# First batch of a fused attention and feed-forward kernel: k and q loaded as rows, normalised there, turned by TensorE

## The chip, the cores and the metric

One core of one Trainium2 chip runs the whole program. Its engines are TensorE (PE, with its weight loads PEld), VectorE (DVE), ScalarE (ACT), GpSimd (POOL) and SyncE (SP), which here issues every DMA, one after the other. The metric is the device time of one execution in microseconds; the kernel before took 1610.94 us (median of 3 runs, 1608.66 to 1612.02).

## The reference

Inputs: q, k, v of 8 batches x 12 heads x 448 tokens x 64 numbers, two gains of 64 numbers, and the weights of a feed-forward layer (768 x 2048 and 2048 x 768, float64 in DRAM, so that each weight has to be put together from two 32-bit halves on the core). Cut to what matters:

```python
q_n = q / sqrt(mean(q*q, -1) + 1e-6) * g_q      # the same for k with g_k
scores = q_n @ k_n.T / 8                         # per batch and head, 448 x 448
attn = softmax(scores)                           # max subtracted, sum + 1e-9
x = (attn @ v) as [8*448 tokens, 12*64]
h = x @ w_in
out = (s * relu(h)**2 + b) @ w_out               # 3584 x 768
```

## The kernel before, in words

**Precision.** TensorE multiplies in fp32r; where that is not enough a number is split into a rounded high part and the rest, and two or three products are added up. So k lies on 128 partitions as its high part (64 rows) over its low part (`ka`), q twice as its high part (`qa`), and the low part of q stands in `qb`, with one more row for the negated maximum of each query; `kb` is the high part of k with a row of ones.

**Pairs and slots.** The 96 heads are worked in 48 pairs (6 pairs are one batch); `j` is the head within a pair. The first part of the program is one loop over slots. A slot does one 128-key chunk of one head: two matmuls into `st` (`score_t`, L343 and L346), its exponent on ACT (L358 in the first batch, L362 later), and two slots later its product with v (`weigh`, L402). A pair has W = 8 slots, so slot 0 to slot 383 are attention. Ten slots ahead (AHEAD) a slot also makes one 112-query block of plain scores `sh` (L305), whose row maximum DVE takes (L316).

**What each pair needs first.** A table `jobs` says in which slot, counted from the pair's first slot s0 = 8p (s1 = s0 + 4j), each preparation stands: `load` brings k and q of the pair as rows (`raw`, 448 KB), `norm` squares them on ACT (L242), sums on DVE (L247) and raises the mean to -1/2 on POOL (L249, L250); `keep` writes these 1/rms to DRAM, `spread` reads them back onto all 128 partitions (`rb`, 448 KB for each head), `load_kq` brings k and q of a head a second time, already turned and on 128 partitions (`kq`, 448 KB), `scale` multiplies the two (L267, L268) and `split_kq` makes `ka`, `qa`, `qb` (L286 to L290). `double_kb` copies the high part of k into `kb` by a DMA, `shift` puts the maxima into `qb` by a DMA, `take`, `gather` and `divide` (L427 to L443) form the softmax's division through DRAM, `split_x` makes the operand of the feed-forward layer.

**The rest.** `convert` turns the 24 pieces of w_in (512 KB each) from float64 into a high and a low part: one load (L119), two ACT instructions, four on DVE, one on POOL. PACE lists the slots in which it goes on. Its load buffer `w64` exists once. From slot START + 48b on, `filler` gives TensorE the feed-forward matmuls of the batch just finished, FILL = (2, 2, 2) of them in each slot (L175); before the first such slot TensorE has attention alone. `rectify` takes their sums out (L192) and stores them (L194). After the loop the last batch's w_in matmuls run while w_out is converted, and then all the w_out matmuls (L621).

**What sets the order.** In the first part all five engines run in exactly the order in which the program is written (`manual_schedule`), SP among them: an instruction that waits holds up all behind it on its engine. Within a slot the order is: `score_t`, two filler matmuls, the last exponent's split, the exponent, jobs begun in an earlier slot, the jobs of this slot in order of the pair, the plain score and two filler matmuls, `rectify`, `split_e_lo`, the maximum, the weight pieces, `weigh`, two filler matmuls.

Of the kernel before, what the change touches and what calls it, by code (L numbers as in the profile page):

```python
# [23 lines left out]
START = 16  # L24
# [3 lines left out]
FIRST = -31  # L28
# [3 lines left out]
PACE = (-24, *range(2, 62, 5), *range(60, 93, 3))  # L32
# [5 lines left out]
def attention_then_relu2_ffn(  # L38
# [3 lines left out]
    kq_rows: bass.AP,  # L42
    v: bass.AP,
# [6 lines left out]
):  # L50

# [14 lines left out]
    nc = tc.nc  # L66
# [120 lines left out]
    def rectify():  # L187

        while later:
            ph, bank, b, fc = later.pop(0)  # L190
            r = xp.tile([P, SEQ], F32, tag="r", bufs=2, name=f"r{b}_{fc}")
            S.activation(r, ph[:, :SEQ], AF.Relu)  # L192
            free.append(bank)
            nc.sync.dma_start(r_d[b][fc], r)  # L194

    with tc.tile_pool(name="apool", bufs=1) as ap:
        raws, kqs, invs, vrs, nmxs, shs = ({} for _ in range(6))
        sts, movers, avs, uzs, zts, zbs, us = ({} for _ in range(7))

        def load(p):  # L200
            raw = raws[p] = ap.tile([P, 2, TILES, D], F32, tag="raw", name=f"raw{p}")
            nc.sync.dma_start(raw, kq_rows[p])

# [60 lines left out]
        def scale(p, j):  # L264
            t, rb = kqs[p, j], invs.pop((p, j))
            engine = V if p < NP else G
            engine.tensor_tensor(t[:, 0], t[:, 0], rb[:, 0], ALU.mult)  # L267
            V.scalar_tensor_tensor(t[:, 1], t[:, 1], gqk, rb[:, 1], ALU.mult, ALU.mult)  # L268
# [13 lines left out]
        def split_kq(p, j):  # L282

            t, n = kqs.pop((p, j)), p % 2
            a = slice(j * SEQ, (j + 1) * SEQ)
            S.copy(ka[n][:, a], t[:, 0])  # L286
            S.copy(qa[n][:, a], t[:, 1])
            G.tensor_tensor(ka[n][D:, a], t[D:, 0], ka[n][D:, a].bitcast(F32), ALU.subtract)  # L288
            engine = V if p < NP else G
            engine.tensor_tensor(qb[n][:D, a], t[:D, 1], qa[n][:D, a].bitcast(F32), ALU.subtract)  # L290
# [81 lines left out]
        def split_e_lo(i):  # L372
            p, j, kc, rows = chunk(i)
            if p < NP:
                return
            st, bank = sts.pop(i)
            ah = movers[i][0]
            if kc < 3:
                al = ap.tile([P, SEQ], F32R, tag="al", bufs=3, name=f"al{i}")
                movers[i].append(al)  # L380
            else:
                al = ah[rows:]
            V.tensor_tensor(al, st[:rows, :SEQ], ah[:rows].bitcast(F32), ALU.subtract)  # L383
            free.append(bank)
# [135 lines left out]
        for i, s_ in enumerate(chain((-29,), PACE)):  # L520
            for n in range(1 + 3 * (i > 0)):
                at(s_ + n, next, converted, None)
# [9 lines left out]
        with tc.manual_schedule(engines=ORDERED):  # L532
            begun = []
            for s_ in range(FIRST, NSLOT + START + 1):
                if s_ == FIRST + 3:
# [5 lines left out]
                if s_ in (-28, -20, -13):  # L541
                    warm_up(30)
# [7 lines left out]
                begun = [g for g in begun if next(g, 0) is None]  # L550
                for f, a in jobs[s_]:
# [26 lines left out]
            rectify()  # L578


    with tc.tile_pool(name="opool", bufs=2) as op:
# [57 lines left out]
        with tc.manual_schedule(engines=ORDERED - {ENGINE.SP}):  # L639
# [4 lines left out]
            for m in range(NFC + NFC // NS):  # L644
# [8 lines left out]
                for step in range(4):  # L653
                    for g in now:
                        next(g)
                    if step == 1:
                        rectify()
                    if step == 2:
# [54 lines left out]
```

## Time and profile before

| what | value |
|---|---|
| median of 3 runs | 1610.94 us |
| profiled execution, its own time | 1612.49 us |
| its span on the core | 1610.7 us |
| mean granted TensorE clock | 0.956 |
| PE busy over the span | 1477.9 us, 92% |
| DVE, ACT, POOL busy | 58%, 50%, 46% |
| first feed-forward matmul starts | 227.8 us |

The page's strip of 40 slices is about 40 us a slice: the first five or six slices, the slots without feed-forward matmuls, are the ones in which PE is not at 9. In rows of the timeline the first two numbers are the start in the span and the duration, and the bracket at the end is the idle time of the engine just before with what ended it. In rows of waits the three numbers are the total, how often, and the longest. In the table by windows the numbers are busy us of each engine, then the granted clock, the DMA share and GB/s.

### The profile page before, as it was taken

How to read it: one execution, taken by the hardware profiler on the slowest of the kernel's cores; microseconds unless marked ns; L12 is line 12 of the kernel's file. 1: busy time of each engine (PE TensorE's matmuls, PEld its weight loads, DVE VectorE, ACT ScalarE, POOL GpSimd, SP SyncE). 2: the span in 40 equal slices, each digit the busy share in tenths (PEclk: the TensorE clock that was granted, in tenths of full speed). 3: DMA queues.
4: the chain of work that ended last, by engine and by line, in shares of the span. 5: the costliest groups of instructions: out<-in, count | busy, mean ns of one | idle time of the engine just before them, and what ended most of it. 6: DMA issues, size and time to landing. Idle time of an engine off the chain costs nothing. (4 is left out here: it accounts for less than half of the span.)

```text
span 1610.7 us, 21747 instructions
## 1 busy us (share of the span) xinstructions
PE 1477.9 (92%) x7344; PEld 1354.8 (84%) x7344; DVE 939.8 (58%) x1405; ACT 804.8 (50%) x1504; POOL 743.0 (46%) x599
## 2 busy tenths in 40 slices
PE   6666558999999999999999999999799999999998
PEld 6444447989989989989888989998699999999998
DVE  4687778677777777777677767349943222222210
ACT  2444546666666667666666666525632222222210
POOL 5456666767767767767666766115620000000000
PEclk8878779999999999999999999999899999999999
DMA  5666646665665666656656654166633323232310
GB/s 172 192 187 194 177 139 181 200 187 175 186 184 183 183 181 182 187 177 187 182 177 183 184 179 140 55 190 196 185 108 97 84 82 99 72 108 73 90 38 30
DMA packets 226240, 241.92 MB, mean 150 GB/s; under 512 B 74832, under 2 KB 201808, under 8 KB 226128
## 3 DMA queue, kind: packets, MB, share of 16 engines
q1 hardware_dynamic: 226128, 240.53, 50.3%
q8 instruction: 58, 0.95, 0.3%
q14 instruction: 54, 0.44, 0.1%
HBM read 188.22 MB, written 40.89 MB: 142 GB/s over the span
## 5 line engine op out<-in xcount | busy, mean ns | idle before, releaser
L175 PE MATMUL ph<-x,wih 128*128 128x448 f32 x1536 | 491.8, 368 | 0.0
L175 PEld LDWEIGHTS ph<-x,wih 128*128 128x128 f32 x1536 | 292.9, 191 | 23.5
L362 ACT ACTIVATE st<-st 128x448 f32<-128x448 f32 x336 | 176.9, 526 | 255.5 <-PE st L346 253.5
L316 DVE TENSOR_REDUCE nmx<-sh 112x1 fp32r<-112x448 f32 x384 | 236.9, 618 | 111.9 <-PE sh L305 109.0
L175 PE MATMUL ph<-x,wil 128*128 128x448 f32 x768 | 285.9, 372 | 0.0
L621 PE MATMUL po<-woh,gh 128*128 128x384 f32 x896 | 231.3, 337 | 10.3 <-ACT gh L608 8.7
L621 PE MATMUL po<-wol,gh 128*128 128x384 f32 x896 | 230.8, 337 | 2.0 <-POOL wol L134 2.0
L621 PE MATMUL po<-woh,gl 128*128 128x384 f32 x896 | 229.7, 337 | 1.0 <-DVE gl L609 1.0
L402 PE MATMUL av<-ah,vs 128*128 128x448 f32 x672 | 197.4, 376 | 12.5 <-ACT ah L370 7.6
L305 PE MATMUL sh<-ka,qa 128*112 128x448 f32 x384 | 150.1, 394 | 55.7 <-POOL ka L288 49.9
L288 POOL TENSOR_TENSOR ka<-kq,ka 64x448 fp32r<-64x448 f32 x96 | 114.6, 1194 | 175.7 <-ACT ka L286 170.9
L383 DVE TENSOR_TENSOR al<-st,ah 128x448 fp32r<-128x448 f32 x252 | 155.1, 616 | 60.3 <-ACT ah L370 60.3
L370 ACT CAST ah<-st 128x448 fp32r<-128x448 f32 x336 | 179.1, 533 | 2.4
L621 PEld LDWEIGHTS po<-woh,gh 128*128 128x128 f32 x896 | 163.5, 190 | 12.0 <-ACT gh L608 9.3
L621 PEld LDWEIGHTS po<-wol,gh 128*128 128x128 f32 x896 | 163.5, 190 | 3.2 <-POOL wol L134 3.2
L305 PEld LDWEIGHTS sh<-ka,qa 128*112 128x112 f32 x384 | 107.8, 282 | 69.2 <-POOL ka L288 60.7
L343 PE MATMUL st<-qa,ka 128*128 128x448 f32 (+1 forms) x384 | 165.0, 430 | 1.0 <-DVE nmx L316 1.0
L621 PEld LDWEIGHTS po<-woh,gl 128*128 128x128 f32 x896 | 163.1, 189 | 1.4 <-DVE gl L609 1.4
L175 PEld LDWEIGHTS ph<-x,wil 128*128 128x128 f32 x768 | 146.5, 191 | 12.2
L346 PE MATMUL st<-qb,kb 128*128 128x448 f32 (+1 forms) x384 | 147.0, 383 | 2.2 <-DMA qb<-nmx 2.2
L402 PEld LDWEIGHTS av<-ah,vs 128*128 128x128 f32 x672 | 129.8, 194 | 22.8 <-ACT ah L370 13.3
L603 ACT ACTIVATE r<-r 128x2048 f32<-128x2048 f32 x28 | 53.7, 1917 | 172.1 <-DMA r<-r_d 172.1
(66 smaller groups left out, 2125.2 us busy)
## 6 DMA issues: line engine op xcount, KB each, us to landing
kq<-in_dram SPq DMA_DIRECT2D x96, 448.0 KB, 4.1
rb<-i_d SPq DMA_DIRECT2D x96, 448.0 KB, 5.0
r_d<-r SPq DMA_DIRECT2D x128, 224.0 KB, 3.8
r<-r_d SPq DMA_DIRECT2D x24, 1024.0 KB, 5.9
raw<-in_dram SPq DMA_DIRECT2D x48, 448.0 KB, 4.8
w64i<-in_dram SPq DMA_DIRECT2D x24, 512.0 KB, 4.9
w64o<-in_dram SPq DMA_DIRECT2D x48, 256.0 KB, 3.1
kb<-ka SPq DMA_DIRECT2D x96, 112.0 KB, 2.8
```

The costliest lines, as they stand in the source:

```text
L175: T.matmul(ph[:, :SEQ], w[:, cc, f0 : f0 + P], xs[b, cc][:, part, :], start=n == 0, stop=n == 3 * NCC - 1,)
L288: G.tensor_tensor(ka[n][D:, a], t[D:, 0], ka[n][D:, a].bitcast(F32), ALU.subtract)
L305: T.matmul(sh[:QC, :SEQ], qa[p % 2][:, a].rearrange("k (p c) -> k c p", c=NQ)[:, c], ka[p % 2][:, a], start=True, stop=True,)
L316: V.tensor_reduce(out=nmxs[p][:, c : c + 1], in_=sh[:QC, :SEQ], op=ALU.max, axis=AX.X, negate=True)
L343: T.matmul(st[:rows, :SEQ], ka[n][:, keys], qa[n][:, q], start=True, stop=False)
L346: T.matmul(st[:rows, :SEQ], kb[n][:, keys], qb[n][:, q], start=False, stop=True,)
L362: S.activation(st[:rows, :SEQ], st[:rows, :SEQ], AF.Exp)
L370: S.copy(ah[:rows], sts[i][0][:rows, :SEQ])
L383: V.tensor_tensor(al, st[:rows, :SEQ], ah[:rows].bitcast(F32), ALU.subtract)
L402: T.matmul(av[:, :SEQ], x, a, start=kc == 0 and m == 0, stop=kc == 3 and m == len(todo) - 1,)
L603: S.activation(r, r, AF.Square)
L621: T.matmul(po[e][0][:, :HALF], x[:, fc, :], w[:, f, e * HALF : (e + 1) * HALF], start=fc == 0 and m == 0, stop=fc == NFC - 1 and m == 2,)
```

## The change

- For the six pairs of the first batch k and q are loaded once, as rows of a new input `rows0` (112 partitions, 224 KB for each head, `load_rows`). `norm_rows` squares on ACT into another tile, sums on DVE, forms 1/rms on POOL for 112x8 numbers and multiplies the rows by it on POOL. `turn` lets TensorE transpose the eight 112x64 blocks of a head into two PSUM tiles; `split_turned` makes `ka`, `qa`, `qb` from PSUM with three ACT and two DVE instructions (the gain goes in there). `load`, `norm`, `keep`, `load_kq`, `spread`, `scale` and `split_kq` are no longer done for these pairs; later pairs keep them.
- For later pairs `load_kq` and `spread` stand one slot later by the table, and `double_kb` one slot later for all.
- The four steps of `divide` move from s0 + 14, 15, 18, 21 to s0 + 13, 14, 16, 18. START goes from 16 to 13, FIRST from -31 to -22, and PACE's slots move with them by one for most pieces. Only two groups of warm-up matmuls of 30 remain of three.
- The stores of `r` are issued at the start of the jobs of the next slot (`keep_r`), no longer right behind the ACT instruction that makes `r`.
- The low part `al` of an exponent has two buffers, before three (the squares of `norm_rows` use them as well).

```diff
-START = 16
+START = 13
-FIRST = -31
+FIRST = -22
-PACE = (-24, *range(2, 62, 5), *range(60, 93, 3))
+PACE = (-17, *range(1, 61, 5), *range(59, 92, 3))
...
             S.activation(r, ph[:, :SEQ], AF.Relu)
             free.append(bank)
+            kept.append((b, fc, r))
+    def keep_r():
+        while kept:
+            b, fc, r = kept.pop(0)
             nc.sync.dma_start(r_d[b][fc], r)
...
+        def load_rows(p, j):
+            tag = f"{('kq', 'rb')[p % 2]}{j}"
+            raw = raws[p, j] = ap.tile([QC, 2, NQ, D], F32, tag=tag, name=f"rows{p}_{j}")
+            nc.sync.dma_start(raw, rows0[p, :, j])
+        def norm_rows(p, j):
+            raw = raws[p, j].rearrange("p t c d -> p (t c) d")
+            n = 2 * NQ
+            sq = ap.tile([QC, n, D], F32, tag="al", bufs=2, name=f"sq{p}_{j}")
+            S.activation(
+                sq.rearrange("p i d -> p (i d)"), raw.rearrange("p i d -> p (i d)"), AF.Square
+            )
+            yield
+            ssq = ap.tile([QC, n], F32, tag="ssq", bufs=2, name=f"ssq{p}_{j}")
+            V.tensor_reduce(out=ssq, in_=sq, op=ALU.add, axis=AX.X)
+            ri = ap.tile([QC, n], F32, tag="ri", bufs=2, name=f"ri{p}_{j}")
+            G.tensor_scalar(ri, ssq, 1.0 / D, 1e-6, ALU.mult, ALU.add)
+            G.tensor_tensor(ri, ri, mhalf[:QC, :n], ALU.pow)
+            G.tensor_tensor(raw, raw, ri.unsqueeze(2).broadcast_to([QC, n, D]), ALU.mult)
+        def turn(p, j):
+            raw = raws.pop((p, j))
+            for t in range(2):
+                tk, bank = psum(f"tk{p}_{j}_{t}")
+                for c in range(NQ):
+                    T.transpose(
+                        tk[:D, c * QC : (c + 1) * QC], raw[:, t, c], ident[:QC, :QC]
+                    )
+                tks[p, j, t] = tk[:D, :SEQ], bank
+        def split_turned(p, j):
+            n, a = p % 2, slice(j * SEQ, (j + 1) * SEQ)
+            (k, k_bank), (q, q_bank) = (tks.pop((p, j, t)) for t in range(2))
+            S.copy(ka[n][:D, a], k)
+            S.activation(qa[n][:D, a], q, AF.Copy, scale=gqk[:D])
+            S.activation(qa[n][D:, a], q, AF.Copy, scale=gqk[:D])
+            yield
+            V.tensor_tensor(ka[n][D:, a], k, ka[n][:D, a].bitcast(F32), ALU.subtract)
+            V.scalar_tensor_tensor(
+                qb[n][:D, a], q, gqk[:D], qa[n][:D, a].bitcast(F32), ALU.mult, ALU.subtract
+            )
+            free.extend((k_bank, q_bank))
...
-                al = ap.tile([P, SEQ], F32R, tag="al", bufs=3, name=f"al{i}")
+                al = ap.tile([P, SEQ], F32R, tag="al", bufs=2, name=f"al{i}")
...
-            at(s0 - 30, load, p)
-            at(s0 - 26, norm, p)
-            at(s0 - 22, keep, p)
+            if p >= NP:
+                at(s0 - 30, load, p)
+                at(s0 - 26, norm, p)
+                at(s0 - 22, keep, p)
...
-                at(s1 - 19 if p else -27, load_kq, p, j)
-                at(s1 - 19 if p else -19, spread, p, j)
-                at(s1 - 14, scale, p, j)
-                at(s1 - 12, split_kq, p, j)
-                at(s1 - 11, double_kb, p, j)
+                if p >= NP:
+                    at(s1 - 18, load_kq, p, j)
+                    at(s1 - 18, spread, p, j)
+                    at(s1 - 14, scale, p, j)
+                    at(s1 - 12, split_kq, p, j)
+                else:
+                    at(max(s1 - 28, FIRST), load_rows, p, j)
+                    at(s1 - 20, norm_rows, p, j)
+                    at(s1 - 13, turn, p, j)
+                    at(s1 - 12, split_turned, p, j)
+                at(s1 - 10, double_kb, p, j)
...
-            at(s0 + 14, divide, p, 0)
-            at(s0 + 15, divide, p, 1)
-            at(s0 + 18, divide, p, 2)
-            at(s0 + 21, divide, p, 3)
+            at(s0 + 13, divide, p, 0)
+            at(s0 + 14, divide, p, 1)
+            at(s0 + 16, divide, p, 2)
+            at(s0 + 18, divide, p, 3)
...
-                if s_ in (-28, -20, -13):
+                if s_ in (FIRST, FIRST + 4):
                     warm_up(30)
```

How the rows move shows at two places. The first is ACT at the program's start. Before (raw is a pair's rows, kq a head turned, wih and w64i a piece of w_in):

```order
L242 ACTIVATE raw_211<-raw_211 128x896
L123 ACTIVATE wih_213<-w64i_215 128x512
L133 CAST wih_213<-wai_216 128x512
L123 ACTIVATE wih_213<-w64i_265 128x512
L242 ACTIVATE raw_270<-raw_270 128x896
L286 CAST ka_190<-kq_0_251 128x448
L287 CAST qa_192<-kq_0_251 128x448
```

Of the changed kernel (rows_0 and rows_1 are the two heads of a pair, tk what TensorE has turned):

```order
L225 ACTIVATE sq_0_253<-rows_0_244 112x512
L125 ACTIVATE wih_248<-w64i_250 128x512
L225 ACTIVATE sq_1_298<-rows_1_246 112x512
L135 CAST wih_248<-wai_251 128x512
L125 ACTIVATE wih_248<-w64i_302 128x512
L249 CAST ka_190<-tk_0_0_318 64x448
L250 ACTIVATE qa_192<-tk_0_1_323,gqk 64x448
L251 ACTIVATE qa_192<-tk_0_1_323,gqk 64x448
L225 ACTIVATE sq_0_331<-rows_0_255 112x512
```

The first split of k (L286, now L249) stood behind two pairs' squares and the second piece of w_in; it now stands behind two heads' squares and the same second piece.

The second place is SP (the DMA queue) in a later batch, over the steps that lead to the division of pair 15 (zt15 gathered, z_d15 written). Before:

```order
L435 DMA zb14_3623<-z_d14_96 64x448 x2
L293 DMA qb1_197<-nmx17_3526 1x112x4
L253 DMA i_d19_149<-ri19_3545 128x2x7
L202 DMA raw20_3632<-in_1_dram 128x896
L194 DMA r_d1_75<-r1_5_3638 128x448
L419 DMA zt15_3515<-uz15_1_3626 64x1x7
L293 DMA kb0_194<-ka0_190 64x448
L206 DMA kq19_0_3709<-in_0_dram 128x2x448
L262 DMA rb19_0_3711<-i_d19_149 128x2x448
L194 DMA r_d1_75<-r1_6_3717 128x448
L293 DMA qb1_197<-nmx17_3526 1x112x4
L431 DMA z_d15_97<-zt15_3515 128x7
```

Of the changed kernel:

```order
L308 DMA i_d19_149<-ri19_3663 128x2x7
L212 DMA raw20_3752<-in_1_dram 128x896
L204 DMA r_d1_75<-r1_6_3758 128x448
L472 DMA zt15_3628<-uz15_1_3741 64x1x7
L204 DMA r_d1_75<-r1_7_3831 128x448
L484 DMA z_d15_97<-zt15_3628 128x7
L346 DMA qb1_197<-nmx17_3644 1x112x4
L346 DMA kb0_194<-ka0_190 64x448
L261 DMA kq19_0_3857<-in_0_dram 128x2x448
L317 DMA rb19_0_3859<-i_d19_149 128x2x448
L472 DMA zt16_3852<-uz16_0_3850 64x1x7
```

Between the second gather of a pair and the writing of its quotients stood five other transfers, with `load_kq` among them; now one store of `r` stands there, and `load_kq` comes behind.

More of the change, by code (lines that the diff above doesn't have):

```diff
@@ L42, in attention_then_relu2_ffn @@
     kq_rows: bass.AP,
+    rows0: bass.AP,
     v: bass.AP,
@@ L193, in rectify @@
             free.append(bank)
+            kept.append((b, fc, r))
+    kept = []
+    def keep_r():
+        while kept:
+            b, fc, r = kept.pop(0)
             nc.sync.dma_start(r_d[b][fc], r)
     with tc.tile_pool(name="apool", bufs=1) as ap:
-        raws, kqs, invs, vrs, nmxs, shs = ({} for _ in range(6))
+        raws, kqs, invs, vrs, nmxs, shs, tks = ({} for _ in range(7))
         sts, movers, avs, uzs, zts, zbs, us = ({} for _ in range(7))
@@ L265, in scale @@
             t, rb = kqs[p, j], invs.pop((p, j))
-            engine = V if p < NP else G
-            engine.tensor_tensor(t[:, 0], t[:, 0], rb[:, 0], ALU.mult)
+            G.tensor_tensor(t[:, 0], t[:, 0], rb[:, 0], ALU.mult)
             V.scalar_tensor_tensor(t[:, 1], t[:, 1], gqk, rb[:, 1], ALU.mult, ALU.mult)
@@ L288, in split_kq @@
             G.tensor_tensor(ka[n][D:, a], t[D:, 0], ka[n][D:, a].bitcast(F32), ALU.subtract)
-            engine = V if p < NP else G
-            engine.tensor_tensor(qb[n][:D, a], t[:D, 1], qa[n][:D, a].bitcast(F32), ALU.subtract)
+            G.tensor_tensor(qb[n][:D, a], t[:D, 1], qa[n][:D, a].bitcast(F32), ALU.subtract)
         def move(to, of):
@@ L519, in attention_then_relu2_ffn @@
                 at(W * NP * (b + 1) + START - 2 + k_, split_x, b, k_)
-        for i, s_ in enumerate(chain((-29,), PACE)):
+        for i, s_ in enumerate(chain((FIRST + 1,), PACE)):
             for n in range(1 + 3 * (i > 0)):
@@ L534, in attention_then_relu2_ffn @@
             for s_ in range(FIRST, NSLOT + START + 1):
-                if s_ == FIRST + 3:
+                if s_ == FIRST:
                     nc.sync.dma_start(gg, g_qk)
@@ L550, in attention_then_relu2_ffn @@
                 begun = [g for g in begun if next(g, 0) is None]
+                keep_r()
                 for f, a in jobs[s_]:
@@ L578, in attention_then_relu2_ffn @@
             rectify()
+            keep_r()
     with tc.tile_pool(name="opool", bufs=2) as op:
@@ L657, in attention_then_relu2_ffn @@
                         rectify()
+                        keep_r()
                     if step == 2:
@@ L697 @@
     g = _np.stack([_np.tile(_np.asarray(inputs[x]), 2) for x in ("g_q", "g_k")], 1)
-    laid = [kq, rows, vs, g] + [_np.asarray(inputs[x]) for x in _INS]
+    rows0 = _np.stack([a[0].reshape(n // b, 2, 4, s // 4, d) for a in (k, q)], 2)
+    rows0 = rows0.transpose(0, 4, 1, 2, 3, 5)
+    laid = [kq, rows, rows0, vs, g] + [_np.asarray(inputs[x]) for x in _INS]
     arrays, args = {}, []
```

## The prediction

> **What bounds the kernel now.** The page's strip first: PE at 9 is the sign that nothing else matters, and it stands there from the seventh slice.
>
> ```profile
> PE   6666558999999999999999999999799999999998
> ```
>
> The six slices before it are the first batch's attention, with no feed-forward matmul to fill in. The table by windows says who is busy there, and in a later batch:
>
> ```profile
> 36.00:127.00 91.00, 59.05 (x166) 37.59 (x164) 70.36 (x102) 39.13 (x76) 43.15 (x36) 0.80 0.68 201
> 127.00:220.00 93.00, 53.96 (x156) 36.80 (x156) 67.56 (x95) 44.27 (x89) 63.87 (x50) 0.78 0.56 166
> 480.00:560.00 80.00, 78.23 (x377) 71.47 (x376) 58.71 (x91) 54.63 (x113) 56.07 (x45) 0.98 0.60 184
> ```
>
> In the front PE is busy 65% and 58%, DVE 77% and 73%, and no engine is full: it is held by waits that pass from queue to queue. Later PE is full, and a microsecond saved elsewhere is worth nothing. The waits of the two front windows, first of 36 to 127, then of 127 to 228:
>
> ```profile
> PE sh L305 <- POOL ka L288: 26.2, 5, 6.5
> ACT wih L123 <- DMA w64i<-in_dram: 14.4, 6, 4.3
> ...
> ACT wih L123 <- DMA w64i<-in_dram: 17.0, 6, 6.3
> PE sh L305 <- POOL ka L288: 14.7, 4, 6.3
> ```
>
> The first score of a head waits for the low part of k from POOL. The clock to measure by is the exponent (one a slot) and the first feed-forward matmul; the exponents of slots 0, 31 with 32, and 59, and that matmul:
>
> ```profile
> 42.21 0.53 ACT L358 ACTIVATE e<-st 128x448 f32<-128x448 f32 x1
> 126.78 0.96 ACT L358 ACTIVATE e<-st 128x448 f32<-128x448 f32 x2
> 208.35 0.51 ACT L362 ACTIVATE st<-st 64x448 f32<-64x448 f32 x1 [3.72 <-PE st L346]
> 227.82 0.57 PE L175 MATMUL ph<-x,wih 128*128 128x448 f32 x1
> ```
>
> So 42.2 us pass before slot 0, then 85.0 (2.66 a slot) to slot 32, 81.1 (27 slots, 3.0 each) to slot 59, and 19.5 to the filler. From there on the time is PE's work, so the forecast is a sum over these four stretches.
>
> **Stretch 1, up to the exponent of slot 0.** The old chain in its rows, from load to first score:
>
> ```profile
> 4.48 0.95 ACT L242 ACTIVATE raw<-raw 128x896 f32<-128x896 f32 x1 [2.26 <-DMA raw<-in_dram]
> 8.00 3.05 POOL L250 TENSOR_TENSOR ri<-ri,mhalf 128x14 f32<-128x14 f32 x1
> 9.38 0.34 SPq L119 DMA_DIRECT2D w64i<-in_dram  x1
> 13.56 0.70 ACT L123 ACTIVATE wih<-w64i 128x512 fp32r<-128x512 f32 x1 [2.81 <-DMA w64i<-in_dram]
> 19.49 0.63 DVE L267 TENSOR_TENSOR kq<-kq,rb 128x448 f32<-128x448 f32 x1 [1.14 <-DMA rb<-i_d]
> 24.13 1.18 PE L305 MATMUL sh<-ka,qa 128*112 128x448 f32 x4 [0.60 <-POOL ka L288]
> ```
>
> From the end of the power (11.05) to the scaled k (20.1) it goes through DRAM: 9 us. The change replaces that by a product on POOL (about 1.3 us), eight transposes (1.7) and copies. What is late next is the second piece of w_in: it stands ahead of the first split on ACT (the order rows of the change), and its load starts only when DVE has read the first piece. That was at 9.38, with the data at 13.56; the row loads now go ahead of the pieces, but the 448 KB `kq` loads do not compete, so I leave it there. 13.6 + 0.7 (square) + three copies of 0.55 + 0.6 on DVE gives a first score at 16.5, 7.6 earlier. From the first score to the exponent were 18.1 us, spent on two further heads' preparation and the transfer of the maxima; the same walk now (four maxima of 0.6 with the second head's split between them, the transfer of 4.7, two scores) ends at about 30. **Gain 12**, bounds 6 (the pieces' load later by 6) and 15.
>
> ```profile
> qb<-nmx SPq DMA_DIRECT2D x96, 1.8 KB, 4.7
> w64i<-in_dram SPq DMA_DIRECT2D x24, 512.0 KB, 4.9
> ```
>
> **Stretch 2, slots 0 to 32.** Groups of 36 to 127, nine heads' preparation:
>
> ```profile
> L268 DVE SCALAR_TENSOR_TENSOR kq<-kq,gqk,rb 128x448 f32<-128x448 f32 x9 | 11.2, 1247 | 0.0
> L267 DVE TENSOR_TENSOR kq<-kq,rb 128x448 f32<-128x448 f32 x9 | 9.4, 1042 | 2.4 <-DMA rb<-i_d 2.4
> L290 DVE TENSOR_TENSOR qb<-kq,qa 64x448 fp32r<-64x448 f32 x9 | 8.0, 894 | 5.4 <-ACT qa L287 5.3
> L247 DVE TENSOR_REDUCE ssq<-raw 128x14 f32<-128x896 f32 x4 | 4.3, 1076 | 1.5 <-ACT raw L242 1.5
> L250 POOL TENSOR_TENSOR ri<-ri,mhalf 128x14 f32<-128x14 f32 x4 | 12.1, 3021 | 0.3
> L288 POOL TENSOR_TENSOR ka<-kq,ka 64x448 fp32r<-64x448 f32 x8 | 11.0, 1379 | 16.3 <-ACT ka L286 15.2 <-DMA qb<-nmx 0.8
> L134 POOL TENSOR_TENSOR wil<-wai,wih 128x512 fp32r<-128x512 f32 x8 | 11.1, 1381 | 9.3 <-ACT wih L133 9.0
> L286 ACT CAST ka<-kq 128x448 fp32r<-128x448 f32 x8 | 4.5, 562 | 0.0
> ...
> L383 DVE TENSOR_TENSOR al<-st,ah 128x448 fp32r<-128x448 f32 x14 | 8.6, 615 | 0.6 <-ACT ah L370 0.6
> ...
> 1.61 21.93 PE L212 MATMUL warmth<-ident 128*128 128x128 f32 x180 [1.61 <-POOL ident masks.py:199]
> ```
>
> - DVE loses 11.2 + 9.4 + 8.0 + 4.3 = 32.9. It gains per head a sum over 512 numbers (1.08 x 512/896 = 0.62) and two subtractions that read PSUM; the nearest row, L383 (36 to 245), reads PSUM and took 0.615, as the high end L290 took 0.89. With 0.62 and 0.65: 1.9 x 9 = 17. DVE's 70.4 become 54.5.
> - POOL loses the 11.0 of L288 and 12.1 of powers; it gains per head the power (3.02 x 8/14 = 1.7), 0.2 ahead of it, and the product over 512 numbers (1.38, as L134): 3.3 x 9 = 30. Its 43 become 50 of 91, still half idle.
> - ACT gains per head a third copy and keeps the rest, some 6 in all: 45 of 91.
> - PE gains eight transposes a head. No transpose is in the trace; 90 warm-up matmuls of 128 columns (180 records) took 21.93, 0.244 each, so 112 columns 0.21 and eight 1.7, 15 for nine heads. Below it could be half (one record instead of two); above, twice (half clock).
>
> Two ways to the length. DVE keeps its share: 85.0 x 54.5/70.4 = 66. Or by PE: minus 26.2 of waits for `ka`, plus 15 of transposes, minus the slow matmuls behind each long wait. After such a wait matmuls run at half rate for some 3 us, as the first row here shows against the second:
>
> ```profile
> 90.45 0.73 PE L305 MATMUL sh<-ka,qa 128*112 128x448 f32 x1 [5.88 <-POOL ka L288]
> 249.22 0.37 PE L343 MATMUL st<-qa,ka 128*128 128x448 f32 x1
> 249.42 0.36 PE L346 MATMUL st<-qb,kb 128*128 128x448 f32 x1
> ```
>
> Five such waits cost about 1.7 each, 8.5 together, so 65. The loads of w_in (4.9 us into one buffer, every third or fourth slot) keep some of their 14.4, so I take 68. **Gain 17**; bounds 5 (all load waits stay and transposes cost double) and 24 (DVE 90% busy).
>
> The Trainium skill (Perfetto Trace Analysis, "Optimizing Scalar/DVE Operations") warns that GpSimd and VectorE share an SBUF read port, so that moving work between them might not help; by it the nine new products on POOL, 12 us, would lie on DVE too, and the gain would be about 5 instead of 17. The rows bear out the contention (L267's mean of 1.04 against 0.63 in the single row above), but 11.0 us of `ka` on POOL leave at the same time, so I count it as even. For a transpose of 128x128 its page VectorE: DVE Perf Modes ("The three transpose paths") gives 390 ns, of bf16; by that, an estimate, the nine heads' would be 25 instead of 15.
>
> **Stretch 3, slots 32 to 59.** Nothing that is added is left here. What changes is SP: `load_kq` and `double_kb` come a slot later, when their buffer or source is ready, and block less that stands behind. In 127 to 228 SP's waits are led by:
>
> ```profile
> SPq L206 <- POOL qb L290: 21.7, 6, 6.4
> ```
>
> Some part of that reaches ACT through late pieces; SP's waits for the single load buffer of the pieces stay. **Gain 5**, bounds -5 and 15.
>
> **Stretch 4, to the filler.** The filler may start at slot 61, not 64. Of 19.5 us the last two slots before it take some 9, so 10.5 are saved; the attention of three slots moves under the filler, 3 x 5.75 matmuls of 0.205 (249.22 to 249.42) = 3.5; and of the pieces' waits about 3 move beneath it. **Gain 4**, bounds 0 and 10.
>
> **Later batches.** PE stays full: 11.75 matmuls x 0.205 = 2.41 a slot, and the transfers must only be in time. The division moves one slot up, which costs the gather of its sums 2.4 us of cover, and there is little:
>
> ```profile
> 511.14 0.51 ACT L362 ACTIVATE st<-st 64x448 f32<-64x448 f32 x1 [1.03 <-PE st L346]
> 514.74 0.49 SPq L419 DMA_DIRECT2D zt<-uz  x1
> 519.25 0.17 DVE L427 TENSOR_SCALAR zt<-zt 128x7 f32<-128x7 f32 x1 [1.98 <-DMA zt<-uz]
> ...
> SPq L206 <- POOL qb L290: 157.8, 63, 4.3
> SPq L194 <- ACT r L192: 139.9, 47, 7.4
> ```
>
> The exponent of slot 11 of that pair, some 0.3 behind the slot's start, is at 511.14; its gather is issued at 514.74, 3.9 behind the start, and DVE waits 1.98 for it. The last two rows (SP, 245 to 1110) say why: SP is held by the old `load_kq` and the stores of `r`. Both move by a slot. In the new order SP has four or five issues of 0.5 in the slot before, so the gather leaves about 1.5 behind its slot, 2.4 better, which is just what the earlier division takes. Zero, bounds -10 and 10.
>
> **Sum.** 12 + 17 + 5 + 4 = 38. The profiled execution took 1612.5, 1.6 over the median of the runs shown, so 1574.5 for it and 1573 against the median. I predict **1574**.
>
> **Rivals.**
> - *The pieces of w_in become the wait* (18%). What was hidden behind `ka` shows: SP issues a piece's load behind rows that wait for `turn`, and ACT and DVE stop for it. For it: the load rows above, 31 us of ACT's waits already. Against: per head 224 KB of loads compete with them, where 1,120 did (half of `raw`, `kq`, `rb`). Stretch 2 then keeps its 14.4 and takes 80 instead of 68, stretch 3 gains nothing: 38 - 12 - 5 = 21, so 1590.
> - *More goes* (14%). The front comes to PE's own pace: stretch 2 at 62 (6 more) and stretch 3 at 2.5 a slot instead of 2.8, another 9, with 4 in stretch 4: 57, so 1554.
> - *Slower: the division's wait* (6%). If SP's lag stays 3.9, each pair from the seventh on finds its sums 2.4 later, DVE stands 4.4 instead of 2.0, and `al` and the maxima behind it come too late for PE. About 1.2 can be borne, as L268 no longer follows in the same slot; 1.2 x 42 pairs = 50, so 1573 + 50 = 1623. It decides from 0.9 us a pair.
> - *Nothing moves* (4%): the saved front is given back by stalls of 38 under the filler, 1611.
>
> **How the numbers follow.** My forecast has 58%, with a range of its own of 1562 to 1586. The range of 8 in 10 adds most of both neighbours: 1553 to 1600. About 0.2% (3 us) is what a measurement tells from none: faster 0.90, same 0.04, slower 0.06.
>
> **What would show it.** First exponent at 28 to 33; L288's waits gone from the first batch, and the first score of a head not waiting over 2 us; slot 32 near 98; the first feed-forward matmul near 185; a later batch still at some 19.2 us a pair with DVE's wait for `zt` near 2 us. It is wrong if PE waits for `tk`'s splits or ACT for w64i as long as for `ka` now, or if the waits of `av` for `al` grow from 24 us over the later batches:
>
> ```profile
> PE av L402 <- DVE al L383: 24.0, 18, 4.0
> ```

## The result, and the profile after

The changed kernel takes 1565.11 us (median of 4 runs, 1563.07 to 1565.91) where the kernel before took 1609.80 on the same chip (4 runs, 1608.08 to 1612.02): a ratio of 0.972, 95% interval 0.9703 to 0.9737. That is 44.7 us less, where 38 were forecast. The profiled execution of the changed kernel took 1564.78 us, its span 1563.0.

The page's strip of the changed kernel, 39 us a slice; PE now reaches 9 in the seventh slice; before it was in the eighth, not in the seventh as the forecast has it:

```profile
PE   8775679999999999999999999997999999999998
```

Its table by windows, slots 0 to 32 and slots 32 to 59 (the columns are as before):

```profile
30.00:103.00 73.00, 58.12 (x227) 39.51 (x226) 65.87 (x97) 46.63 (x89) 46.37 (x45) 0.93 0.47 129
103.00:182.00 79.00, 49.24 (x143) 31.57 (x141) 63.56 (x85) 41.20 (x83) 58.13 (x45) 0.81 0.64 184
```

DVE, busy 77% of the first stretch before, is now busy 90% of a shorter one.

Its timeline at the start, and then the rows by which the stretches are measured (exponents of slots 0, 31 with 32, and 59, and the first feed-forward matmul):

```profile
1.61 16.11 PE L267 MATMUL warmth<-ident 128*128 128x128 f32 x120 [1.61 <-POOL ident masks.py:199]
15.78 0.69 ACT L125 ACTIVATE wih<-w64i 128x512 fp32r<-128x512 f32 x1 [2.72 <-DMA w64i<-in_dram]
17.55 0.93 PE L241 MATMUL tk<-ident,rows 112*64 112x112 f32 x8
18.14 0.53 ACT L249 CAST ka<-tk 64x448 fp32r<-64x448 f32 x1 [1.67 <-PE tk L241]
19.91 0.54 PE L358 MATMUL sh<-ka,qa 128*112 128x448 f32 x1 [1.43 <-ACT qa L251]
30.58 0.55 ACT L411 ACTIVATE e<-st 128x448 f32<-128x448 f32 x1 [2.45 <-PE st L399]
...
102.46 0.98 ACT L411 ACTIVATE e<-st 128x448 f32<-128x448 f32 x2
181.16 0.52 ACT L415 ACTIVATE st<-st 64x448 f32<-64x448 f32 x1
185.66 0.57 PE L177 MATMUL ph<-x,wih 128*128 128x448 f32 x1
```

The first turn stands right behind the warm-up matmuls, and the first copy waits for it, not for the piece of w_in (15.78). The waits of the two stretches, 30 to 103 and then 103 to 186:

```profile
PE sh L358 <- DVE ka L253: 10.2, 5, 3.9
ACT wih L125 <- DMA w64i<-in_dram: 6.9, 6, 2.6
...
ACT wih L125 <- DMA w64i<-in_dram: 14.7, 6, 5.0
PE sh L358 <- POOL ka L342: 10.3, 4, 5.3
```

The 26.2 us that PE waited for `ka` from POOL in the first stretch have become 10.2 from DVE. Starts of slots' exponents, read from the timelines of seven kernels (us; the runs are told below):

| | before | changed | START and division old | these and SP's order old | before with the new START and division | one warm-up, piece later | without the product |
|---|---|---|---|---|---|---|---|
| slot 0 | 42.2 | 30.6 | 29.3 | 29.3 | 43.3 | 28.6 | 28.8 |
| slot 32 | 127.2 | 102.9 | 103.4 | 103.8 | 124.8 | 100.1 | 98.3 |
| slot 64 | 233.6 | 207.6 | 203.2 | 205.9 | 229.1 | 204.5 | 201.8 |
| slot 72 | 263.7 | 236.1 | 237.7 | 238.0 | 258.5 | 233.0 | 230.3 |
| slot 383 | 1039.0 | 997.9 | 995.5 | 1008.1 | 1018.7 | 992.1 | 990.2 |
| 72 to 383 | 775.3 | 761.8 | 757.9 | 770.1 | 760.2 | 759.1 | 759.9 |

The two profiled executions differ by 47.7 us: 27.6 of them are there at slot 72, 13.5 more come in slots 72 to 383, which were forecast at zero, and 6.6 lie behind slot 383. The place of the 13.5 is the batch boundary, where `split_x` makes the next operand of the feed-forward layer. Before, in the timelines of DVE and PE, and then in the table by windows:

```profile
357.53 0.17 DVE L427 TENSOR_SCALAR zt<-zt 128x7 f32<-128x7 f32 x1 [1.97 <-DMA zt<-uz]
357.86 1.69 DVE L268 SCALAR_TENSOR_TENSOR kq<-kq,gqk,rb 128x448 f32<-128x448 f32 x1
359.46 2.11 DVE L452 TENSOR_TENSOR x<-u,x 128x448 fp32r<-128x448 f32 x2
361.50 0.61 DVE L383 TENSOR_TENSOR al<-st,ah 128x448 fp32r<-128x448 f32 x1
...
362.16 0.47 PE L402 MATMUL av<-al,vs 128*128 128x448 f32 x1 [1.77 <-DVE al L383]
```

```profile
362.00:367.00 5.00, 4.84 (x16) 4.33 (x17) 4.99 (x10) 3.26 (x7) 3.20 (x2) 0.66 0.02 4
```

The first division step waits for its sums, the scaling of q and two subtractions of `split_x` follow in the same slot, `al` comes late, PE stands 1.77 us, and then five microseconds run at a mean clock of 0.66. In the changed kernel, PE's timeline and the window:

```profile
331.92 0.65 PE L455 MATMUL av<-ah,vs 128*128 128x448 f32 x2 [1.58 <-DVE ah L436]
335.29 0.47 PE L455 MATMUL av<-al,vs 128*128 128x448 f32 x1 [0.48 <-DVE al L436]
```

```profile
332.00:337.00 5.00, 4.52 (x21) 3.78 (x22) 4.96 (x10) 3.15 (x7) 1.40 (x2) 1.00 0.14 47
```

The stall is still there, 1.58 us, but the clock stays whole. What goes with this is seen between the marks at which the granted clock can change: in every one of the 14 traces its changes lie a whole number of 3.413 us apart. The next rows of the table by windows run from mark to mark. The first three are of the kernel before: the window with a boundary's stall, the window behind it, and one with the larger part of a later boundary's stall that a mark cuts in two. The last is of the changed kernel, a window with a boundary's stall:

```profile
359.90:363.31 3.41, 1.64 (x9) 1.19 (x8) 3.41 (x5) 1.62 (x4) 0.65 (x1) 1.00 0.57 182
363.31:366.73 3.42, 3.42 (x11) 3.00 (x10) 3.42 (x7) 3.25 (x7) 2.93 (x2) 0.50 0.03 5
841.20:844.60 3.40, 2.14 (x11) 2.02 (x12) 3.40 (x7) 1.45 (x4) 0.58 (x1) 1.00 0.19 68
447.15:450.56 3.41, 1.83 (x10) 1.39 (x10) 3.37 (x5) 2.88 (x7) 3.22 (x3) 1.00 0.04 15
```

Over slots 100 to 383 of all 14 traces the clock fell 12 times, each time behind a window in which PE was busy 1.42 to 1.65 us of the 3.41. Of some 2,800 windows behind which it stayed whole, one had 1.63 and all others 1.78 or more. A stall of 1.58 us leaves at least 1.83, so it never reached that far; one of 1.77 leaves 1.64 where it lies between two marks, and more where a mark cuts it, as at 841 us.

### The profile page after: what moved, and what is told of

It reads as the page before. It is cut to its first block, busy times and chain, and to the rows that moved or that the text cites. A ratio compares the mean times of both kernels' runs of the same rounds, so it can differ in the third digit from the quotient of the medians.

```text
span 1563.0 us, 21722 instructions
## 1 busy us (share of the span) xinstructions
PE 1466.8 (94%) x7380; PEld 1347.0 (86%) x7380; DVE 904.3 (58%) x1399; ACT 816.0 (52%) x1522; POOL 735.6 (47%) x611
## 5 line engine op out<-in xcount | busy, mean ns | idle before, releaser
L683 PEld LDWEIGHTS po<-woh,gh 128*128 128x128 f32 x896 | 162.7, 189 | 10.6 <-ACT gh L670 7.1
L396 PE MATMUL st<-qa,ka 128*128 128x448 f32 (+1 forms) x384 | 160.6, 418 | 5.5 <-DVE nmx L369 4.5
L496 POOL TENSOR_TENSOR u<-uz,zb 64x448 f32<-64x448 f32 x96 | 118.2, 1231 | 59.7 <-DMA zb<-z_d 55.9
L342 POOL TENSOR_TENSOR ka<-kq,ka 64x448 fp32r<-64x448 f32 x84 | 98.8, 1176 | 98.2 <-ACT ka L340 85.6
```

Of the source, the lines that this page charges most:

```text
L396: T.matmul(st[:rows, :SEQ], ka[n][:, keys], qa[n][:, q], start=True, stop=False)
L496: G.tensor_tensor(u[a], uzs.pop((p, j))[a], zb[a], ALU.mult)
L683: T.matmul(po[e][0][:, :HALF], x[:, fc, :], w[:, f, e * HALF : (e + 1) * HALF], start=fc == 0 and m == 0, stop=fc == NFC - 1 and m == 2,)
```

## The experiments

Each was timed against the kernel before on the chip it ran on; ratios are to that, with their 95% interval.

### Where the later batches' gain comes from

**START alone back.**

```diff
-START = 13
+START = 16
```

> The changed kernel with START back at 16 and nothing else: the feed-forward matmuls begin at slot 64 and the split of x stands at slots 6, 7, 0 of a pair again, while the division keeps its new slots (13, 14, 16, 18). To be explained are the 15 us that the later batches gained (slot 64 to 383: 805.3 us before, 790.3 after). Theory A (at each batch boundary the split of x, the first step of the division and the scaling of q came in one slot on DVE, and PE went to half clock behind them): the coincidence of the three needs the old division slots as well, so the boundary stays without its long stall, the later batches keep most of the gain, and only the three slots of cover are lost, 0 to 6 us: 1565 to 1571. If the place of the split of x alone decides, 1578 to 1585. Theory B (SP's order brings the 15 us): 1565 to 1571, slot 64 to 383 near 790.

Measured: 1563.18 us, 0.9702 (0.9685 to 0.9718). That is a little under the 1565 to 1571 that both theories gave, so this run does not tell them apart. Slots 64 to 383 took 791.0. The later batches keep their gain and the three slots of cover are worth nothing that can be told: with START = 13 there are 18 feed-forward matmuls fewer behind slot 383 (371 against 389), but slots 60 to 64 take 23.8 us against 18.4 here. DVE's wait for the sums, 61.8 us in the changed kernel (240 to 960), rose to 94.9 here (same window), while PE's waits for `al` and the last chunk's low part fell from 14.5 to 8.2: the wait for the sums does not by itself cost PE anything.

**START and the division back.**

```diff
-START = 13
+START = 16
-            at(s0 + 13, divide, p, 0)    # and 14, 16, 18
+            at(s0 + 14, divide, p, 0)    # and 15, 18, 21
```

> The changed kernel with START = 16 and the division at its old slots 14, 15, 18, 21, so that split of x, first division step and scaling of q meet in one slot of DVE at each batch boundary as before. Theory A (the meeting costs the 15 us): slot 64 to 383 takes 803 to 808 us again and the clock is about 0.66 in the 5 us behind each boundary; with the lost three slots of cover 1580 to 1586. Theory B (SP's order): 1565 to 1572, slot 64 to 383 near 790.

Measured: 1568.73 us, 0.9738 (0.9723 to 0.9753). Theory A falls: the three meet in one slot again, and slots 72 to 383 take 757.9. Its boundary, in PE's timeline and by window:

```profile
333.40 0.48 PE L455 MATMUL av<-al,vs 128*128 128x448 f32 x1 [1.51 <-DVE al L436]
```

```profile
333.00:338.00 5.00, 4.20 (x19) 3.58 (x20) 5.00 (x9) 3.29 (x9) 2.96 (x2) 1.00 0.25 81
```

PE stands 1.51 us where it stood 1.77, and the clock holds. DVE waits 0.64 us there for the sums of the division, where it waited 1.97 before.

**SP's order back.**

```diff
-                    at(s1 - 18, load_kq, p, j)     # and spread
+                    at(s1 - 19, load_kq, p, j)
-                at(s1 - 10, double_kb, p, j)
+                at(s1 - 11 if p >= NP else s1 - 10, double_kb, p, j)
-            kept.append((b, fc, r))
+            nc.sync.dma_start(r_d[b][fc], r)
```

> The changed kernel with SP's old places for later pairs: the loads of kq and rb in slot -19, the copy into kb in slot -11, the stores of r issued right behind the instruction that makes r. Theory A (the phase of DVE's work at the batch boundary): the later batches stay as they are, 1564 to 1568. Theory B (SP's order): slot 64 to 383 goes back to 803 to 808 and the time to 1578 to 1582. My forecast's own argument on SP was that the later gather's lag falls from 3.9 us by some 2.4 through these moves; if that is what the earlier division lives on, DVE's wait for zt grows here from 2.0 us per pair to some 4.4, and the kernel loses 10 to 50 us.

Measured: 1561.42 us, 0.9696 (0.9681 to 0.9712), slots 72 to 383 in 758.1. Theory B falls too. So does my own argument that the earlier division lives on SP's new order; DVE's wait for the sums did not grow (240 to 960; 61.8 in the changed kernel):

```profile
DVE zt L480 <- DMA zt<-uz: 49.5, 29, 3.3
```

**Before, with START, the division and PACE new.**

```diff
-START = 16
+START = 13
-PACE = (-24, *range(2, 62, 5), *range(60, 93, 3))
+PACE = (-24, *range(1, 61, 5), *range(59, 92, 3))
-            at(s0 + 14, divide, p, 0)    # and 15, 18, 21
+            at(s0 + 13, divide, p, 0)    # and 14, 16, 18
```

> The kernel before with START = 13, the division at 13, 14, 16, 18 and the pieces of w_in one slot earlier, nothing of the row path and nothing of SP's order. Theory A: the later batches gain their 15 us here too, and three slots of filler lie under the front (4 us): 1588 to 1594, slot 64 to 383 near 790. Theory B (SP's order): only the 4 us, 1604 to 1608; and if the earlier gather without SP's moves stalls DVE, slower than before, 1612 to 1650.

Measured: 1590.07 us, 0.9873 (0.9858 to 0.9888). With nothing of the row path, slots 72 to 383 fall from 775.3 to 760.2. So the new phase (START and the division's slots) is enough in the kernel before, and yet is not needed in the changed one. That leaves one reading: either of the two edits alone cures the boundary, and only with both old does it cost. The next two runs test it.

**Phase and SP's order both back**, that is, the row path alone (the edits of the second and third run together).

> The changed kernel with START 16, the old division slots and all three old places on SP together; only the row path of the first batch, the two buffers of al and PACE stay changed. Slots 72 to 383 took 775.3 us before and 757.9 to 761.8 in every kernel that changed either the phase of DVE's work or SP's order. Theory C (either change alone is enough to keep PE's stall at the batch boundary short of the drop to half clock): with both undone the stall is 1.77 us again with half clock for some 3.4 us behind it, slots 72 to 383 take 773 to 777, and the time is 1578 to 1588. Rival (the rest of the change, al's two buffers or the memory that the row path frees, brought it): 757 to 763 and 1563 to 1570.

Measured: 1585.01 us, 0.9861 (0.9827 to 0.9894): theory C, some 20 us over the changed kernel. Slots 72 to 383 took 770.1, under the 773 to 777 of the theory; the profiled execution was the fastest of its four, so this is a low value.

**The same, with the stores of r left at their later place.**

```diff
-START = 13
+START = 16
+            ... division, load_kq, spread, double_kb at their old slots; keep_r stays
```

> As the run before, but the stores of r keep their later place; only the loads of kq and rb and the copy into kb stand at their old slots on SP, with START 16 and the old division. If the earlier loads are what delays the gather of the softmax sums (DVE's wait for zt 1.97 us at the boundary before, 0.64 with the later loads): slots 72 to 383 at 773 to 777 and 1578 to 1588. If the stores of r right behind their instruction are what delays it: 757 to 763 and 1563 to 1570.

Measured: 1585.54 us, 0.9854 (0.9813 to 0.9895), slots 72 to 383 in 774.1. Its boundary, in the timelines of DVE and PE and by window, is that of the kernel before, row by row:

```profile
451.92 0.53 DVE L480 TENSOR_SCALAR zt<-zt 128x7 f32<-128x7 f32 x1 [1.63 <-DMA zt<-uz]
452.60 1.68 DVE L322 SCALAR_TENSOR_TENSOR kq<-kq,gqk,rb 128x448 f32<-128x448 f32 x1
454.20 2.11 DVE L505 TENSOR_TENSOR x<-u,x 128x448 fp32r<-128x448 f32 x2
...
456.90 0.47 PE L455 MATMUL av<-al,vs 128*128 128x448 f32 x1 [1.79 <-DVE al L436]
```

```profile
457.00:462.00 5.00, 5.00 (x17) 4.47 (x18) 4.99 (x9) 3.26 (x7) 3.46 (x2) 0.66 0.02 6
```

DVE's wait for the sums is 1.63 us again. The later stores of `r` play no part; with the old phase it is the slot of the loads and of the copy into `kb` that decides. Which of the three transfers it is was not tried apart.

### What holds up the first batch

**One group of warm-up matmuls, and the second piece of w_in later.**

```diff
-                if s_ in (FIRST, FIRST + 4):
+                if s_ == FIRST:
-PACE = (-17, ...)
+PACE = (-14, ...)
```

> The changed kernel with one group of 30 warm-up matmuls instead of two and the first entry of PACE at -14 instead of -17, so that the second piece of w_in comes behind the first split of k on ACT. My forecast held that this second piece sets the first score; the trace shows the turn of the first head held by the warm-up matmuls until 17.55 us although its rows were ready at 11.06. If both hold in turn, the first score falls from 19.91 to 14 or 15 us, the exponent of slot 0 from 30.6 to 25 or 26, and the whole from 1565 to 1560 or 1561. Rival (the walk from the first score to the exponent, held by the second head and the transfer of the maxima, takes up what is gained, or PE is slower without its warm-up): exponent of slot 0 at 29 to 31, and the time stays within 2 us.

Measured: 1562.78 us, 0.9712 (0.9687 to 0.9737): no different from the changed kernel that can be told. Its start, in rows of PE, ACT and SP:

```profile
13.20 0.57 PE L358 MATMUL sh<-ka,qa 128*112 128x448 f32 x1 [1.40 <-ACT qa L251]
...
16.47 0.69 ACT L125 ACTIVATE wih<-w64i 128x512 fp32r<-128x512 f32 x1 [2.16 <-DMA w64i<-in_dram]
17.07 0.51 ACT L249 CAST ka<-tk 64x448 fp32r<-64x448 f32 x1
...
22.46 0.58 SPq L346 DMA_DIRECT2D qb<-nmx  x1
...
28.65 0.54 ACT L411 ACTIVATE e<-st 128x448 f32<-128x448 f32 x1 [3.75 <-PE st L399]
```

The first score comes 6.7 us earlier, but the exponent of slot 0 comes neither at the 25 or 26 of the theory nor at the 29 to 31 of the rival: the piece now stands ahead of the second head's split, the maxima leave at 22.46, and of the 6.7 us 1.9 are left at slot 0, 2.8 at slot 32 (100.07) and 3.1 at slot 64. The forecast of the next run goes by 0.2 at slot 32; that was the exponent of slot 33, at 102.73.

**The piece later still.**

```diff
-PACE = (-17, ...)
+PACE = (-4, ...)       # one warm-up group, as above
```

> The changed kernel with one group of 30 warm-up matmuls and the first entry of PACE at -4, so that the second piece of w_in comes behind the splits of both heads of pair 0 and behind the maxima of the first head. With the entry at -14 the first score came at 13.20 us and the exponent of slot 0 still only at 28.65, since the piece then stood ahead of the second head's split on ACT and of the fourth maximum on DVE (the maxima left at 22.46). Theory (the piece is handed from head to head): the fourth maximum now ends near 21, the transfer leaves at 21 and the exponent of slot 0 comes at 26 to 27; slots 0 to 32 unchanged at 72 to 74, the time 1559 to 1562. Rival (the start is not worth anything, since slots 0 to 32 give it back: with -14 the exponent of slot 0 was 2.0 earlier and slot 32 only 0.2): slot 32 at 102 to 104 and 1562 to 1566.

Measured: 1564.09 us, 0.9705 (0.9674 to 0.9737). Slot 0 at 28.0, slot 32 at 103.0, slot 64 at 206.6: the rival, though what it built on, the 0.2 at slot 32, was misread. Here the 2.6 us won at slot 0 are gone at slot 32. In the nine kernels with the row path that keep the product on POOL, slot 0 comes at 28.0 to 32.3 and slot 32 at 100.1 to 104.7. Among the eight that start by 30.7 the earliest start (this run) has a slot 32 no earlier than the changed kernel's, and the earliest slot 32 belongs to the third start: the start goes with it only loosely.

**The product of the rows on ACT.**

```diff
-            G.tensor_tensor(raw, raw, ri.unsqueeze(2).broadcast_to([QC, n, D]), ALU.mult)
+            yield
+            for i in range(n):
+                S.activation(raw[:, i], raw[:, i], AF.Copy, scale=ri[:, i : i + 1])
```

> The changed kernel with the product of the rows with 1/rms on ACT, as eight instructions of 112x64 a slot later, instead of one of 112x512 on POOL. In the changed kernel one DVE instruction of every piece of w_in takes 2.66 us instead of 0.69; each time it begins while POOL works on this product and the low part of w_in back to back. Theory (DVE waits for POOL's two products): the long ones shrink to at most 1.9, the four DVE instructions of a piece sum to about 25 instead of 32 over slots 0 to 32, and these slots shorten from 72.3 to 66 to 69 us if ACT (47 of 73 busy, some 18 more) doesn't take its place; the time 1559 to 1563. Rival (the length comes from something else, or ACT becomes the bound): the 2.66 stay, or slots 0 to 32 take 72 to 80; 1565 to 1573.

The rows that gave the question, DVE's and POOL's timelines of the changed kernel (five of the eight pieces of slots 0 to 32 have such a long row, not every one):

```profile
64.51 0.69 DVE L127 SCALAR_TENSOR_TENSOR wai<-w64i,wai 128x512 int32<-128x512 int32 x1
65.24 2.66 DVE L129 SCALAR_TENSOR_TENSOR wai<-w64i,wai 128x512 int32<-128x512 int32 x1
...
64.90 1.20 POOL L234 TENSOR_TENSOR rows<-rows,ri 112x512 f32<-112x512 f32 x1
66.07 1.28 POOL L136 TENSOR_TENSOR wil<-wai,wih 128x512 fp32r<-128x512 f32 x1
```

Two instructions of the same shape, 0.69 and 2.66 us; the long one ends 0.55 behind the end of POOL's second product (67.35). Measured: 1578.61 us, 0.9816 (0.9787 to 0.9845). The 2.66 us rows are gone (the longest is 1.81), but ACT waits for the power, and PE for ACT; the exponent of slot 0 comes at 39.3 and slots 0 to 32 take 78.1. Waits from 39 to 117:

```profile
ACT rows L236 <- POOL ri L233: 16.4, 7, 5.0
...
PE sh L360 <- ACT uz L466: 13.4, 6, 5.0
```

**The product on DVE**, two slots behind the power:

```diff
-            G.tensor_tensor(raw, raw, ri.unsqueeze(2).broadcast_to([QC, n, D]), ALU.mult)
+            yield
+            yield
+            V.tensor_tensor(raw, raw, ri.unsqueeze(2).broadcast_to([QC, n, D]), ALU.mult)
```

> The changed kernel with the product of the rows with 1/rms on DVE instead of POOL, two slots behind the power. On ACT the product took the 2.66 us rows of DVE away (the longest left is 1.81), and DVE's busy time over the 73 us of slots 0 to 32 fell from 65.9 to 55.0, but ACT held up the uz copies and the time got worse. Theory (POOL's two products back to back hold DVE): DVE pays 0.65 for each of some eight products and gets back about 1.3 to 2.0 for each, so its busy time falls to 56 to 61 and slots 0 to 32 from 72.3 to 66 to 69; the exponent of slot 0 may come up to 2 us later since DVE waits for the power there; the time 1559 to 1564. Rival (DVE's wait for the power takes the place): slots 0 to 32 at 72 to 78 with DVE waiting for ri, 1566 to 1575.

Measured: 1572.29 us, 0.9745 (0.9721 to 0.9769). Slot 0 at 34.5, slots 0 to 32 in 75.7, DVE busy 69.7 of 76 us (34 to 110), not the 56 to 61 expected: the rival's time. Its reason is the smaller part: DVE waited 5.0 us for the power, but the product itself took 1.32 us in the mean, not 0.65, 10.6 for the eight, against 5.9 that the w_in rows got back (26.1, from 32.0). Both moves put the product into an in-order queue that waits for the power, so neither prices the contention alone.

**No product at all.**

```diff
-            G.tensor_tensor(raw, raw, ri.unsqueeze(2).broadcast_to([QC, n, D]), ALU.mult)
```

> The changed kernel without the product of the rows with 1/rms: k and q of the first batch stay unnormalised, the power is still computed but not used; all else is the same. It prices what POOL's product costs through DVE, with nothing put in its place (on ACT and on DVE it cost a wait for the power instead). Theory (the product held DVE, and DVE's share sets slots 0 to 32, so this is the 4 us by which they came out longer than forecast): the 2.66 us rows are gone, DVE's busy time over slots 0 to 32 falls to 54 to 57 from 65.9, these slots shorten from 72.3 to 64 to 69, and the time is 1558 to 1563. Rival (DVE's long rows lie under other waits: the walk from k's split through the score, the maxima and their transfer sets the pace): DVE's busy time falls, but slots 0 to 32 stay at 71 to 74, and the time moves only by what the first score comes earlier (the product's 1.0 to 1.5 us): 1563 to 1566.

Measured: 1559.14 us, 0.9677 (0.9646 to 0.9709). Slot 0 comes 1.8 us earlier and slots 0 to 32 take 69.5 instead of 72.3, just outside the theory's 64 to 69. DVE is busy 62.9 of 70 us (28 to 98), not the 54 to 57 expected: its share stays at 90%, so the theory's direction holds, with a smaller size. DVE's groups from 28 to 97, against those of the changed kernel (30 to 103) and of the kernel before (36 to 127), in this order:

```profile
L127 DVE SCALAR_TENSOR_TENSOR wai<-w64i,wai 128x512 int32<-128x512 int32 x8 | 10.8, 1349 | 0.3
L129 DVE SCALAR_TENSOR_TENSOR wai<-w64i,wai 128x512 int32<-128x512 int32 x8 | 6.4, 795 | 0.3
L132 DVE SCALAR_TENSOR_TENSOR wai<-wih,wai 128x512 f32<-128x512 f32 x8 | 5.8, 731 | 0.0
L124 DVE TENSOR_SCALAR wai<-w64i 128x512 int32<-128x512 int32 x8 | 5.7, 718 | 3.1 <-DMA w64i<-in_dram 3.1
```

```profile
L129 DVE SCALAR_TENSOR_TENSOR wai<-w64i,wai 128x512 int32<-128x512 int32 x8 | 11.4, 1430 | 0.3
L127 DVE SCALAR_TENSOR_TENSOR wai<-w64i,wai 128x512 int32<-128x512 int32 x8 | 7.5, 938 | 0.3
L124 DVE TENSOR_SCALAR wai<-w64i 128x512 int32<-128x512 int32 x8 | 7.2, 897 | 2.3 <-DMA w64i<-in_dram 2.2
L132 DVE SCALAR_TENSOR_TENSOR wai<-wih,wai 128x512 f32<-128x512 f32 x8 | 5.9, 732 | 0.0
```

```profile
L130 DVE SCALAR_TENSOR_TENSOR wai<-wih,wai 128x512 f32<-128x512 f32 x8 | 7.1, 892 | 0.0
L125 DVE SCALAR_TENSOR_TENSOR wai<-w64i,wai 128x512 int32<-128x512 int32 x7 | 4.8, 692 | 0.2
L127 DVE SCALAR_TENSOR_TENSOR wai<-w64i,wai 128x512 int32<-128x512 int32 x7 | 4.8, 691 | 0.2
L122 DVE TENSOR_SCALAR wai<-w64i 128x512 int32<-128x512 int32 x8 | 3.3, 417 | 5.1 <-DMA w64i<-in_dram 5.0
```

The four sum to 28.7, 32.0 and 20.0 us, the last 21.4 if all eight pieces are counted. The product accounts for 3.3 of the 10.6 that were added; the rest stays without it, since the low part of w_in on POOL (L136) alone still meets a DVE instruction.

**SP's old order with the start of the run of one warm-up.** Edits of the third run and of the first one of this part.

> The changed kernel with SP's old places for later pairs, one group of warm-up matmuls and the first entry of PACE at -14. SP's old places alone gave 0.9696 of the time before, the two edits of the start alone 0.9712, the changed kernel 0.972. If the gains add up (the earlier loads of kq and rb relieve slots 40 to 60, where the new start lost the 2 us it had won): 0.966 to 0.968 of the time before, 1556 to 1560, slot 32 at 100 to 103. Rival (slots 0 to 60 run at a pace of their own, whatever the start): 0.969 to 0.972, 1561 to 1565.

The loss in slots 40 to 60 that this names was a misreading too: in the run of one warm-up every slot from 0 to 64 comes 1.4 to 4.6 us earlier than in the changed kernel. Measured: 1559.57 us (4 runs, 1558.78 to 1559.86), 0.9679 (0.9655 to 0.9702), slot 32 at 101.2. It is the fastest of the kernels that compute the reference's result. Its interval just clears that of the changed kernel (0.9703 to 0.9737), which was timed in another session, so the 5.5 us by which it is faster are likely rather than shown.

## Why the prediction was right, and where it was not

The time fell into the predicted range, faster, with 44.7 us against 38. But the sum was right by luck, through errors of opposite sign: the first batch gave less than forecast, and the later batches gave what was put at zero. In the profiled executions the gains were 11.6, 12.7 and 2.9 in stretches 1 to 3, 0.4 in slots 59 to 72, 13.5 up to slot 383 and 6.6 behind it, 47.7 in all. The row path with both phase and SP old (1585.01) is worth some 24.5 us against 1609.52; phase or SP's order, whichever is new, some 16 to 24 more (1568.73 and 1561.42).

- **Stretch 1** (gain 12, measured 11.6; 28 to 33 held, 30.58). The total was right and the reason was not. I had the second piece of w_in set the first score at 16.5; it came at 19.91, because PE was still in its 60 warm-up matmuls, whose own row I had quoted for their duration and not for their place. The walk from first score to exponent took 10.7 where I had about 13.5. The run with one warm-up shows that the piece was next in the line, but also that of a first score 6.7 us earlier only 2 to 3 us last.
- **Stretch 2** (gain 17, measured 12.7: 72.3 instead of 68). The mis-sized term is DVE's busy time: forecast 54.5, measured 65.9, nearly all of the difference in the w_in rows (32.0 against 21.4). I had counted the contention with POOL as even because as much POOL time left as came. It isn't the amount that counts but the meeting: in the changed kernel the two products of POOL stand back to back just when a piece is on DVE. By the Trainium skill's rule I had weighed (Perfetto Trace Analysis, "Optimizing Scalar/DVE Operations") the gain would have been 5; it came out between, nearer to my 17. Of the 4.3 us missing, the run without the product gives back 2.8; the other 1.5 were not traced. Transposes went the other way: eight took 0.93 us at full clock and 1.70 at half, not 1.7 throughout, and scores still wait 10.2 us for `ka`, now from DVE, up to 3.9 at a time where no wait over 2 was forecast.
- **Stretch 3** (gain 5, measured 2.9, 78.3 for slots 32 to 59). It was forecast to come from SP's order, which is not borne out: with the old order slots 32 to 59 took 74.9, and slots 32 to 60 took 82.0 against 80.9 in the changed kernel. SP's wait for `qb` in this stretch fell from 21.7 to 3.8, but ACT's waits for the pieces' loads mostly stayed (14.7, before 17.0).
- **Stretch 4** (gain 4). The first feed-forward matmul came at 185.66, forecast near 185, and that was luck: slot 59 came 6.8 us later than the stretches before it were to bring it (181.16, not 174.4), and the filler 4.5 us behind it, not some 9. And START = 16 put back cost nothing (1563.18): the three slots under the filler made no difference that can be told. What they take from behind the loop, 18 matmuls, is some 3.7 of the 6.6 us gained there; the rest of the 6.6 was not traced.
- **Later batches** (0, bounds -10 to 10; measured 13.5 from slot 72, outside). This is the step that failed. I read the averages, PE full and waits for `al` of 24.0 us in 865, and not where those waits lie: a stall of 1.77 us at every batch boundary, with half clock behind five of the six from slot 100 on. Over slots 72 to 383 the stalls of at least 0.4 us sum to 20.0 before and 15.3 after, and the clock's loss (2 us windows, each times one minus its granted clock) to 8.9 and 3.4; together they are 10.2 of the 13.5. Smaller gaps are not the rest (0.3 and 0.4 in all): between the two exponents that bound this stretch the trace before has 11 matmuls more, 3,643 against 3,632, some 2.2 us at 0.2 each. The run with SP old has 14.7 and 0.0, which makes 14.2 of its 17.2. That 1.51 to 1.58 us left the clock whole and 1.77 often did not goes with how much of one window between two marks stayed idle, as shown with the result; no run set out to move a stall against the marks.
- **The rivals.** The slower one, the earlier division waiting for its sums, did not happen, and with SP's order old it did not either: its premise, that only SP's new order makes room, fell. That the pieces become the wait did not hold in stretch 2, where ACT's waits for their loads fell from 14.4 to 6.9; it held in part at the start, where in the run of one warm-up the second piece took back most of the earlier first score.

## What to carry to other kernels

Look for the boundary events under a busy share of nine tenths: a stall that comes once a batch, with half clock behind it, is worth more than its own length, and two unrelated edits may each shorten it enough to keep the clock whole, so that their gains don't add. In a front of in-order queues that hand work to each other, price an early start at the end of the stretch, not at its beginning. When work moves to POOL, ask which DVE instruction will be running at that moment, not how much POOL does in all.

## What the runs showed of the hardware

- A DVE instruction with its operands in SBUF waits out POOL's elementwise products, two of them where they stand back to back (2.66 us for 0.69), while the maxima, which read PSUM, kept their 0.61 us (608 ns mean in the changed kernel, 611 before). The Trainium skill (SBUF — State Buffer, "Who interferes with whom") says that a DVE instruction with two SBUF inputs contends with a GpSimd (POOL) instruction that reads SBUF, for a port pair that it calls an exclusive lock; the rows agree, and show that POOL's next one can come in between.
- At a batch boundary with a PE stall of 1.76 to 2.28 us the granted clock fell to half for 3.41 us in 12 of 18 cases (the kernel before and the two runs with phase and loads old); with a stall of 1.39 to 1.58 in none of 60 (the ten kernels with phase or loads new and such a stall). It is not the single stall that decides: at slot 74 of the changed kernel (241.5 us) two stalls of 0.86 and 1.47 us together left PE busy 1.64 us between two marks, and the clock was at half for 6.83. The Trainium skill (TensorE: Matmul & The Clock Gate, "What's actually happening") has the clock fall after an idle window of about 3.4 us; here PE was busy 1.42 to 1.65 of the 3.41 us before each of the 12 falls, so a window with half of it idle was enough.
